# Moving the combinations of w_in to VectorE in the last row, with another order of steps in the first and the last pair of tiles

## The chip, the cores and the metric

The kernel runs on one core of a Trainium2 chip. Times are device microseconds of one execution; 0.2% of this kernel's time is 2.3 us. The engines are named as in the profile: PE is TensorE, PEld its weight loads, ACT ScalarE, DVE VectorE, POOL GpSimd, SP the engine that issues the transfers.

## The reference

Three stages follow one another. Attention between 8 batches of 512 tokens (8 heads of 64) and 32 state vectors per head, in both directions, gives 544 rows of 512 numbers per batch. A gated layer (512 to 1536 to 512) and then a second layer (512 to 1024 to 512, with a softmax-weighted activation and a normalisation) work on all rows:

```python
gate = 1.0 / (1.0 + np.exp(-(x @ w_gate)))
x = gate * (x @ w_val) @ w_out
h = x @ w_in
e = np.exp(h - np.max(h, axis=-1, keepdims=True))
solu = h * (e / (np.sum(e, axis=-1, keepdims=True) + 1e-09))
mu, var = mean and variance of solu over a row
out = ((solu - mu) / np.sqrt(var + 1e-06) * g_ln) @ w_out2
```

The weights and two of the outer inputs are 64-bit numbers, which the kernel converts on the chip (class Conv: three steps on VectorE and one integer add on GpSimd per block of 128x512).

## The kernel before

**Precision.** Each operand of a matmul is held as a high and a low half (tiles ...h and ...l, or xe and xo for w_in). A product takes three matmuls (mm3, lines 138 to 140): high by high and the two mixed ones. ScalarE makes the high half with a copy (hi_of, line 129), VectorE or GpSimd the low half with a subtraction (lo_of, line 135; GpSimd on lines 232, 618, 652 and 775).

**The rows.** The first two stages are worked through in nine rows (eight batches of 512 tokens, and one of the 256 state rows), the last of them for batch 7. A row is a loop over twelve chunks of 128 of the 1536 hidden columns (line 1037). In chunk c, TensorE makes the gate's product into the bank gps and the value's into vps (first_mm, 12 matmuls together), and then the output products of chunk c-1 into acc (out_acc, 12 matmuls). ScalarE takes the sigmoid of gps (sigma, L560), VectorE multiplies it with vps (gated, L564), ScalarE and VectorE split the result (gated_hi L129, gated_lo L570). A split of the precomputed state weights for later chunks runs in between (make, mh and ml, L129 and L135). In the last row a step of the conversion of w_out2 is added in chunks 2 to 10 (conv.step): rescaled halves of the block before (woh L234 on ScalarE, wol L235 on VectorE), the two ScalarE reads of the next (L195, L196), three VectorE steps (L203, L206, L213) and the integer add on GpSimd (L223). After the twelfth chunk come a dummy Exp that loads the table (line 1082), the output products of chunk 11, the splits of the four banks of the result (put, line 1085) and the first h products (h2_mm, 24 matmuls for tile 0).

**The steps on w_in.** h = x @ w_in is computed for pairs of 128-row tiles by seven products instead of eight (product, numbers 1 to 7, each of 6 matmuls). They need differences of blocks of w_in: T1 = B12 - B11, T3 = B22 - B12, T2 = B22 - T1 and T4 = B21 - T2, for two halves k of the contraction. w_pair_ops lists the 24 steps for this: 8 joins (high plus low half back to one number), 8 subs and 8 splits (a high half on ScalarE, a low half). The last row takes two of them off the list at the end of each chunk (lines 1079 to 1081), after everything else of that chunk in each engine's queue. Joins, subs and low halves are on GpSimd. The order of the list is written out by hand, and so is that of the row: the engines take their instructions in the order of the program.

**The second layer.** Four tiles of the last row (first) are taken singly, 24 matmuls each; then pairs (line 1128). For a pair, o, v and w are three PSUM banks (banks(i)), used in turn with three others: product 1 goes to o, which is copied to tmp; product 2 to v and v + tmp is tile i's first half of h; products 5 to w, which is copied to tmp (L1149), 6 onto o, copied to u2 (L1151), 3 onto w; w + u2 is tile i's second half. Product 7 goes onto o; o + tmp is the second half of tile i+1 (plus, L696, into v), and product 4 onto o gives its first half. h_max (L693) takes the maxima, chain(i) the exponentials (ScalarE, L716) and statistics (VectorE, L719 to L721), centre(i) subtracts the mean (ScalarE, L728 or L731), turn(i) transposes (VectorE and two transfers through DRAM, lines 762 to 768; on TensorE for the last two tiles, L756), halves(i, q) splits the transposed tile (ScalarE L129, GpSimd L775), row_scale(i) computes the factor of each row (VectorE, and two small instructions on GpSimd), out2(i) multiplies with w_out2 (24 matmuls, in two halves), and store(i) scales and writes. The work on the previous pair, i-2 and i-1, stands between the products of the current one:

```python
            halves(i - 2, 0)
            halves(i - 2, 1)
            row_scale(i - 2)
            product(i, 5, w, True, False)
            act(tmp, w, AF.Copy)
            product(i, 6, o, False, False)
            act(u2, o, AF.Copy)
            product(i, 3, w, False, True)
```

The first pair is i = 4, the last i = 32 (end); for the last, product 7 is issued ahead of chain(i), while the sum of its result stays behind chain(i) and half of the output products of tile i-2.

Of the kernel before, what the change touches and what calls it, by code (L numbers as in the profile page):

```python
# [14 lines left out]
ALU = mybir.AluOpType  # L15
# [11 lines left out]
def attn_moe_moe2_kernel(ctx: ExitStack, tc: tile.TileContext, x, state, w_gate, w_val, w_out, w_in2, w_out2, g_ln, out):  # L27
# [93 lines left out]
    vec = nc.vector  # L121
    pool = nc.gpsimd
    act = nc.scalar.activation

    def r(ap):
        return ap.bitcast(F32)
# [445 lines left out]
    def out_acc(c, n):  # L572
        h, l = woh[c], wol[c]
        i = c % 2
        for m in range(KC):
            sl = slice(m * P, (m + 1) * P)
            mm3(ps_acc(m, n), h[:, sl], l[:, sl], gh[i][:, 0:n], gl[i][:, 0:n], c == 0, c == NF1 - 1)
# [58 lines left out]
    def w_pair_ops(bf):  # L636

        join, sub, split = [{} for _ in range(3)]
        for k in range(2):
            b = dict(zip(("B11", "B12", "B21", "B22"), bf[4 * k:4 * k + 4]))  # L640

            def do_join(n, k=k, b=b):
                h, l = win(k + 2 * (n[1] == "2"), int(n[2]) - 1)
                pool.tensor_tensor(out=b[n], in0=r(h), in1=r(l), op=ALU.add)

            def do_sub(o, x, y, b=b):
                pool.tensor_tensor(out=b[o], in0=b[x], in1=b[y], op=ALU.subtract)

            def do_split(n, x, k=k, b=b):
                h, l = ts[n, k]  # L650
                hi_of(h, b[x])
                pool.tensor_tensor(out=l, in0=b[x], in1=r(h), op=ALU.subtract)

            for n in b:
                join[n, k] = partial(do_join, n)
            for n, x, y in (("T1", "B12", "B11"), ("T3", "B22", "B12"), ("T2", "B22", "B11"), ("T4", "B21", "B22")):
                o = {"T1": "B11", "T3": "B12", "T2": "B22", "T4": "B21"}[n]
                sub[n, k] = partial(do_sub, o, x, y)
                split[n, k] = partial(do_split, n, o)
        steps, late = [], []  # L660
        for k in range(2):
            steps += late[:1] + [join["B11", k], join["B12", k], sub["T1", k], join["B22", k], split["T1", k], sub["T3", k]]
            steps += [sub["T2", k], join["B21", k], split["T3", k], split["T2", k], sub["T4", k]]
            late = [split["T4", k]]
        steps += late
        return steps
# [9 lines left out]
    def h2_out(i, f):  # L676
        if tiles[i][0] == 0:
            return acc[2 * (i % 2) + f]
        a, b, c = banks(i)
        return ((b, c), (a, b))[i % 2][f]  # L680

    def product(i, n, o, start, stop):
        q, b, t = tiles[i]
# [11 lines left out]
    def plus(o, x, y):  # L695
        vec.tensor_tensor(out=o, in0=x, in1=y, op=ALU.add)  # L696
# [313 lines left out]
    with tc.manual_schedule():  # L1010
        for n_b, b in enumerate(blocks[1:], 1):
# [25 lines left out]
            for c in range(NF1):  # L1037
# [39 lines left out]
                elif (b == SREAD or last) and c > 1:  # L1077
                    conv.step(1)
                if last:
                    for _ in range(2):  # L1080
                        w_steps.pop(0)()
        act(stat[0][:, 0:1], half, AF.Exp)
        out_acc(NF1 - 1, S)
        for k in range(KC):
            ends = put(ps_acc(k, S), *yhl(0, k))
        for k in range(KC):
# [40 lines left out]
    with tc.manual_schedule():  # L1127
        for i in range(len(first), nt, 2):
# [13 lines left out]
                store(i - 3)  # L1142
            plus(v, v, tmp)
            h_max(i, 0)
            halves(i - 2, 0)
            halves(i - 2, 1)
            row_scale(i - 2)
            product(i, 5, w, True, False)
            act(tmp, w, AF.Copy)  # L1149
            product(i, 6, o, False, False)  # L1150
            act(u2, o, AF.Copy)  # L1151
            product(i, 3, w, False, True)
            next_ops(q, ops, step, n)
            plus(w, w, u2)
            h_max(i, 1)
            if end:
                product(i, 7, o, False, False)
            chain(i)
            halves(i - 1, 0)
            halves(i - 1, 1)  # L1160
            out2(i - 2, half1)
            if not end:
                product(i, 7, o, False, False)
            plus(v, o, tmp)
            h_max(i + 1, 1)
            centre(i)
            if end:
                product(i, 4, o, False, True)
# [55 lines left out]
```

## Time and profile before

| what | before |
|---|---|
| median of 3 runs | 1135.21 us (1133.67 to 1135.47) |
| profiled execution | 1134.19 us |
| its span, first to last instruction | 1132.4 us |
| mean granted TensorE clock | 0.994 |
| PE busy | 1084.0 us, 96% |
| DVE busy | 766.7 us, 68% |
| ACT busy | 601.8 us, 53% |
| POOL busy | 418.7 us, 37% |

The predictions are made against the profiled execution; its time has 1.8 us outside of the span, and the median of the runs is 1.0 us above it. A timeline row gives the start in us from the beginning of the span, the duration in us, engine, line, operation, written and read tiles, and in brackets the idle time of the engine before it and what ended that. "x2" says that two instructions of one kind in a row are shown as one. The records of neighbouring instructions on an engine overlap by some 0.07 us.

### The profile page before, as it was taken

The numbers are of one execution on the slowest core, as the hardware profiler recorded it, in microseconds if no ns is written. First come the engines' busy times: TensorE is split into PE (matmuls) and PEld (weight loads), VectorE is DVE, ScalarE is ACT, GpSimd is POOL, SyncE is SP. The second block draws the span as 40 slices with busy tenths as digits, with TensorE's granted clock in tenths as the row PEclk, the third lists the DMA queues.
The fourth block names the chain that finished last, engine by engine and source line by source line (L and its number), as shares of the span: only waits on it lengthen the run. The fifth ranks groups of instructions, "written<-read, shape, count | busy, mean of one in ns | idle before, by whom it ended". The sixth has DMA issues, their size and how long they took to land.

```text
span 1132.4 us, 15911 instructions
## 1 busy us (share of the span) xinstructions
PE 1084.0 (96%) x5501; PEld 861.5 (76%) x5501; DVE 766.7 (68%) x1324; ACT 601.8 (53%) x1169; POOL 418.7 (37%) x469
## 2 busy tenths in 40 slices
PE   7887899999999999999999999889999999999998
PEld 5555567778878778778778997667788888888877
DVE  6999865467465575564574466877578778777773
ACT  6766445545444455443555354555565565655552
POOL 2776733300000000000000054676566667667550
PEclk9999999999999999999999999999999999999999
DMA  8763040331440431532412434311453543553431
GB/s 230 258 204 102 20 95 1 80 84 38 116 124 20 115 66 38 164 77 58 96 38 67 142 99 149 106 39 56 134 174 121 174 155 131 164 170 119 158 122 38
DMA packets 139601, 122.89 MB, mean 109 GB/s; under 512 B 71040, under 2 KB 111232, under 8 KB 139520
## 3 DMA queue, kind: packets, MB, share of 16 engines
q1 hardware_dynamic: 139520, 121.87, 36.8%
q8 instruction: 43, 0.70, 0.3%
q14 instruction: 38, 0.31, 0.1%
HBM read 78.32 MB, written 43.52 MB: 108 GB/s over the span
## 4 chain that ended last, share of the span: by engine, by line
PE 73%; DVE 14%; issue 3%; DMA 3%; POOL 2%; ACT 2%; SPq 1%; DVEq 0%; POOLq 0%; ACTq 0%
PE acc L138 10%; PE acc L140 10%; PE acc L139 10%; PE att L138 5%; PE att L140 5%; PE att L139 5%; PE gps L138 4%; PE gps L139 4%; PE gps L140 4%; PE vps L138 4%; PE vps L140 4%; PE vps L139 4%; DVE wf L213 2%; DVE wf L203 1%; DVE wf L206 1%
## 5 line engine op out<-in xcount | busy, mean ns | idle before, releaser
L138 PE MATMUL acc<-gh,woh 128*128 128x512 f32 (+1 forms) x432 | 168.7, 390 | 0.6 <-ACT gh L129 0.6
L564 DVE TENSOR_TENSOR sg<-vps,sg 128x512 f32<-128x512 f32 (+1 forms) x108 | 71.1, 658 | 141.7 <-PE vps L140 123.0
L139 PE MATMUL acc<-gl,woh 128*128 128x512 f32 (+1 forms) x432 | 164.6, 381 | 2.2 <-POOL gl L570 1.3
L140 PE MATMUL acc<-gh,wol 128*128 128x512 f32 (+1 forms) x432 | 164.3, 380 | 0.0
L560 ACT ACTIVATE sg<-gps 128x512 f32<-128x512 f32 (+1 forms) x108 | 61.6, 570 | 154.5 <-PE gps L140 150.0
L138 PEld LDWEIGHTS acc<-gh,woh 128*128 128x128 f32 x432 | 81.8, 189 | 31.9 <-issue 15.5
L256 POOL MEMSET xtr<- 32x256 f32 x18 | 5.4, 302 | 262.1 <-PE att L324 261.5
L139 PEld LDWEIGHTS acc<-gl,woh 128*128 128x128 f32 x432 | 81.9, 190 | 18.5 <-POOL gl L570 2.2
L775 POOL TENSOR_TENSOR wol<-ut,woh 128x512 fp32r<-128x512 f32 x48 | 61.6, 1299 | 87.7 <-ACT woh L129 85.8
L140 PEld LDWEIGHTS acc<-gh,wol 128*128 128x128 f32 x432 | 81.6, 189 | 16.1
L223 POOL TENSOR_TENSOR tt<-tt,xn 128x512 int32<-128x512 int32 x16 | 20.9, 1304 | 194.8 <-DVE tt L213 171.2
L129 ACT ACTIVATE gh<-sg 128x512 fp32r<-128x512 f32 (+1 forms) x101 | 60.5, 599 | 53.6 <-DVE sg L564 53.6
L138 PE MATMUL gps<-ah,mh 128*128 128x512 f32 x192 | 75.9, 396 | 9.3 <-ACT sg L560 4.1
L570 DVE TENSOR_TENSOR gl<-sg,gh 128x512 fp32r<-128x512 f32 (+1 forms) x97 | 76.3, 786 | 10.2 <-ACT gh L129 6.9
L135 DVE TENSOR_TENSOR ml<-gps,mh 64x512 fp32r<-64x512 f32 (+2 forms) x57 | 38.6, 678 | 63.1 <-ACT stg L129 51.0
L138 PE MATMUL att<-woh,woh 128*128 128x512 f32 (+1 forms) x204 | 80.1, 392 | 0.0
L139 PE MATMUL att<-wol,woh 128*128 128x512 f32 (+1 forms) x204 | 79.5, 390 | 0.0
L140 PE MATMUL att<-woh,wol 128*128 128x512 f32 (+1 forms) x204 | 79.5, 390 | 0.0
L129 ACT ACTIVATE mh<-gps 64x512 fp32r<-64x512 f32 (+2 forms) x53 | 31.2, 589 | 90.7 <-PE gps L140 60.4
L139 PE MATMUL gps<-al,mh 128*128 128x512 f32 x192 | 75.4, 393 | 1.7 <-DVE al L135 1.7
L138 PE MATMUL vps<-ah,mh 128*128 128x512 f32 x192 | 75.7, 395 | 1.1 <-DVE ml L135 1.1
L140 PE MATMUL gps<-ah,ml 128*128 128x512 f32 x192 | 75.4, 393 | 1.0 <-DVE ml L135 0.9
(431 smaller groups left out, 2900.0 us busy)
## 6 DMA issues: line engine op xcount, KB each, us to landing
usp<-ub SPq DMA_DIRECT2D x32, 512.0 KB, 2.6
ut<-usp SPq DMA_DIRECT2D x128, 128.0 KB, 2.9
msp<-stg SPq DMA_DIRECT2D x72, 128.0 KB, 2.3
stg<-msp SPq DMA_DIRECT2D x36, 256.0 KB, 2.9
out_dram<-sg SPq DMA_DIRECT2D x32, 256.0 KB, 3.0
xn<-in_x_dram SPq DMA_DIRECT2D x15, 512.0 KB, 5.3
e2t<-in_x_dram SPq DMA_DIRECT2D x96, 64.0 KB, 2.6
stge<-in_moe_w_out_dram SPq DMA_DIRECT2D x10, 512.0 KB, 4.0
```

Of the source, the lines that this page charges most:

```text
L129: return act(dst, src, AF.Copy)
L135: return vec.tensor_tensor(out=dst, in0=src, in1=r(hi), op=ALU.subtract)
L138: mm(o, lh, rh, start=start, stop=False, **kw)
L139: mm(o, lh, rl, start=False, stop=False, **kw)
L140: return mm(o, ll, rh, start=False, stop=stop, **kw)
L203: vec.tensor_scalar(out=t, in0=t, scalar1=EXP_LO, scalar2=EXP_HI, op0=ALU.max, op1=ALU.min)
L213: vec.scalar_tensor_tensor(out=tu, in0=hi, scalar=0xC0000000, in1=tu, op0=ALU.bitwise_and, op1=ALU.bitwise_or)
L223: pool.tensor_tensor(out=ti, in0=ti, in1=lo, op=ALU.add)
L560: act(sg[c % 2][:, 0:n], gps[:, 0:n], AF.Sigmoid)
L564: vec.tensor_tensor(out=g, in0=vps[:, 0:n], in1=g, op=ALU.mult)
L570: eng.tensor_tensor(out=gl[c % 2][:, 0:n], in0=sg[c % 2][:, 0:n], in1=r(gh[c % 2][:, 0:n]), op=ALU.subtract)
L775: pool.tensor_tensor(out=lv, in0=wv[:, 4 * q:4 * q + 4], in1=r(hv), op=ALU.subtract)
```

## The change

1. In w_pair_ops the joins, subs and low halves go from GpSimd to VectorE; the high halves stay on ScalarE.
2. The list of the 24 steps is reordered: the sub of a difference and its split fall into different chunks, T3's sub comes before T1's split, T3's split before B21's join, and T4's split of the first half follows the next B11. In chunk 11 one step is taken instead of two; the last, T4's split, is issued behind the output products of chunk 11.
3. In the first pair (i = 4), halves of tile 2 and row_scale of tile 2 are issued behind the copies to tmp and u2 (between product 6 and product 3) instead of ahead of product 5. In the other pairs nothing moves.
4. In the last pair, the sum of product 7's result goes to the bank acc[3] instead of v, and it and its maximum are issued right behind product 7, ahead of chain(i). h2_out knows the bank.

```diff
--- before.py
+++ after.py
@@ -641,15 +641,15 @@
 
             def do_join(n, k=k, b=b):
                 h, l = win(k + 2 * (n[1] == "2"), int(n[2]) - 1)
-                pool.tensor_tensor(out=b[n], in0=r(h), in1=r(l), op=ALU.add)
+                vec.tensor_tensor(out=b[n], in0=r(h), in1=r(l), op=ALU.add)
 
             def do_sub(o, x, y, b=b):
-                pool.tensor_tensor(out=b[o], in0=b[x], in1=b[y], op=ALU.subtract)
+                vec.tensor_tensor(out=b[o], in0=b[x], in1=b[y], op=ALU.subtract)
 
             def do_split(n, x, k=k, b=b):
                 h, l = ts[n, k]
                 hi_of(h, b[x])
-                pool.tensor_tensor(out=l, in0=b[x], in1=r(h), op=ALU.subtract)
+                vec.tensor_tensor(out=l, in0=b[x], in1=r(h), op=ALU.subtract)
 
             for n in b:
                 join[n, k] = partial(do_join, n)
@@ -659,8 +659,8 @@
                 split[n, k] = partial(do_split, n, o)
         steps, late = [], []
         for k in range(2):
-            steps += late[:1] + [join["B11", k], join["B12", k], sub["T1", k], join["B22", k], split["T1", k], sub["T3", k]]
-            steps += [sub["T2", k], join["B21", k], split["T3", k], split["T2", k], sub["T4", k]]
+            steps += [join["B11", k], *late, join["B12", k], sub["T1", k], join["B22", k], sub["T3", k], split["T1", k]]
+            steps += [sub["T2", k], split["T3", k], join["B21", k], split["T2", k], sub["T4", k]]
             late = [split["T4", k]]
         steps += late
         return steps
@@ -677,7 +677,7 @@
         if tiles[i][0] == 0:
             return acc[2 * (i % 2) + f]
         a, b, c = banks(i)
-        return ((b, c), (a, b))[i % 2][f]
+        return ((b, c), (a, acc[3] if i + 1 == len(tiles) else b))[i % 2][f]
 
     def product(i, n, o, start, stop):
         q, b, t = tiles[i]
@@ -1077,10 +1077,11 @@
                 elif (b == SREAD or last) and c > 1:
                     conv.step(1)
                 if last:
-                    for _ in range(2):
+                    for _ in range(min(2, len(w_steps) - 1)):
                         w_steps.pop(0)()
         act(stat[0][:, 0:1], half, AF.Exp)
         out_acc(NF1 - 1, S)
+        w_steps.pop(0)()
         for k in range(KC):
             ends = put(ps_acc(k, S), *yhl(0, k))
         for k in range(KC):
@@ -1142,27 +1143,36 @@
                 store(i - 3)
             plus(v, v, tmp)
             h_max(i, 0)
-            halves(i - 2, 0)
-            halves(i - 2, 1)
-            row_scale(i - 2)
+            def operand():
+                halves(i - 2, 0)
+                halves(i - 2, 1)
+                row_scale(i - 2)
+
+            if i > len(first):
+                operand()
             product(i, 5, w, True, False)
             act(tmp, w, AF.Copy)
             product(i, 6, o, False, False)
             act(u2, o, AF.Copy)
+            if i == len(first):
+                operand()
             product(i, 3, w, False, True)
             next_ops(q, ops, step, n)
             plus(w, w, u2)
             h_max(i, 1)
             if end:
                 product(i, 7, o, False, False)
+                plus(acc[3], o, tmp)
+                h_max(i + 1, 1)
             chain(i)
             halves(i - 1, 0)
             halves(i - 1, 1)
             out2(i - 2, half1)
             if not end:
                 product(i, 7, o, False, False)
-            plus(v, o, tmp)
-            h_max(i + 1, 1)
+            if not end:
+                plus(v, o, tmp)
+                h_max(i + 1, 1)
             centre(i)
             if end:
                 product(i, 4, o, False, True)
```

## Rows read from the trace of the kernel before

**Rows 1.** The page, part 1: busy us, share of the span, instructions, by engine.
```profile
PE 1084.0 (96%) x5501; PEld 861.5 (76%) x5501; DVE 766.7 (68%) x1324; ACT 601.8 (53%) x1169; POOL 418.7 (37%) x469
```

**Rows 2.** TensorE's waits from 685 to 770 us: total us, times, longest us.
```profile
PE gps L138 <- ACT sg L560: 4.1, 1, 4.1
PE acc L138 <- DVE ml L135: 3.0, 1, 3.0
PE gps L139 <- DVE al L135: 1.1, 2, 0.7
```

**Rows 3.** Window: length, PE, PEld, DVE, ACT, POOL busy (count), PEclk, DMA, GB/s.
```profile
765.00:770.00 5.00, 4.96 (x15) 3.96 (x16) 1.77 (x3) 2.55 (x8) 3.90 (x6) 0.66 0.00 0
```

**Rows 4.** VectorE's timeline, last row: start, duration us, line, operands [idle before].
```profile
684.35 2.79 DVE L135 TENSOR_TENSOR al<-ee,ah 128x512 fp32r<-128x512 f32 x2
...
699.04 0.69 DVE L564 TENSOR_TENSOR sg<-vps,sg 128x512 f32<-128x512 f32 x1 [3.36 <-PE vps L140]
...
704.48 0.69 DVE L564 TENSOR_TENSOR sg<-vps,sg 128x512 f32<-128x512 f32 x1 [1.83 <-PE vps L140]
...
727.46 0.69 DVE L564 TENSOR_TENSOR sg<-vps,sg 128x512 f32<-128x512 f32 x1 [3.81 <-ACT sg L560]
...
728.85 0.69 DVE L570 TENSOR_TENSOR gl<-sg,gh 128x512 fp32r<-128x512 f32 x1
...
731.11 0.69 DVE L213 SCALAR_TENSOR_TENSOR tt<-xn,tt 128x512 uint32<-128x512 uint32 x1
...
740.65 1.79 DVE L570 TENSOR_TENSOR gl<-sg,gh 128x512 fp32r<-128x512 f32 x1
...
744.97 0.69 DVE L213 SCALAR_TENSOR_TENSOR tt<-xn,tt 128x512 uint32<-128x512 uint32 x1
745.58 0.69 DVE L564 TENSOR_TENSOR sg<-vps,sg 128x512 f32<-128x512 f32 x1
...
752.49 0.68 DVE L564 TENSOR_TENSOR sg<-vps,sg 128x512 f32<-128x512 f32 x1
```

**Rows 5.** GpSimd's timeline, last row.
```profile
684.86 3.43 POOL L644 TENSOR_TENSOR bf<-xe,xo 128x512 f32<-128x512 f32 x2
...
740.12 1.76 POOL L647 TENSOR_TENSOR bf<-bf,bf 128x512 f32<-128x512 f32 x1
...
745.80 1.30 POOL L223 TENSOR_TENSOR tt<-tt,xn 128x512 int32<-128x512 int32 x1 [2.21 <-issue]
```

**Rows 6.** ScalarE's timeline, last row.
```profile
726.31 0.63 ACT L129 ACTIVATE T4h<-bf 128x512 fp32r<-128x512 f32 x1 [6.26 <-POOL bf L647]
...
761.63 0.63 ACT L129 ACTIVATE T4h<-bf 128x512 fp32r<-128x512 f32 x1 [3.37 <-POOL bf L647]
```

**Rows 7.** TensorE's timeline, first pair.
```profile
806.87 0.50 PE L138 MATMUL acc<-xe,ys5h 128*128 128x512 f32 x1 [1.14 <-ACT stg L1149]
```

**Rows 8.** ScalarE's timeline, first pair.
```profile
805.19 1.15 ACT L129 ACTIVATE woh<-ut 128x512 fp32r<-128x512 f32 x2 [5.04 <-DMA ut<-usp]
```

**Rows 9.** TensorE's timeline, last pair.
```profile
1101.29 0.39 PE L140 MATMUL att<-woh,wol 128*128 128x512 f32 x1
1103.78 0.52 PE L138 MATMUL acc<-T4h,mh 128*128 128x512 f32 x1 [2.10 <-DVE acc L696]
...
1106.66 0.63 PE L139 MATMUL att<-wol,woh 128*128 128x512 f32 x1
1107.09 0.62 PE L140 MATMUL att<-woh,wol 128*128 128x512 f32 x1
...
1107.78 0.40 PE L139 MATMUL att<-wol,woh 128*128 128x512 f32 x1
...
1115.95 0.60 PE L756 MATMUL gps<-ident,ub 128*128 128x128 f32 x4
```

**Rows 10.** VectorE's timeline, last pair.
```profile
1103.06 0.67 DVE L696 TENSOR_TENSOR acc<-acc,stg 128x512 f32<-128x512 f32 x1
```

**Rows 11.** ScalarE's timeline, last pair.
```profile
1114.25 1.15 ACT L731 ACTIVATE ub<-xn,stat 128x1024 f32<-128x1024 f32 x1
```

## The prediction

> **What bounds the kernel now.** The page comes first: TensorE is busy for 1084.0 us, 96% of the span [rows 1]. Little is left to win, and only where TensorE stands idle or runs at its lower clock. So I read the list of TensorE's waits, limited to the last row (the last pass over the twelve chunks, some 685 to 765 us) [rows 2]: 4.1 us for a sigmoid on ScalarE, 3.0 us for the first split of the row's result, and 1.1 us at its head. These 8.2 us are what the first part of the change can reach, with what they cost behind them. A window shows that price: from 765 to 770 us, behind the 3.0 us, the granted clock is 0.66 [rows 3], that is, mostly the lower level, 1.2 instead of 2.4 GHz.
>
> The timelines of VectorE and GpSimd say why the row is late. At first VectorE waits for TensorE: the gated product of chunk 3 starts 5.44 us after that of chunk 2, TensorE's own pace of 24 matmuls at 0.227 us [rows 4]. From chunk 4 on VectorE sets the pace. The same split takes 0.69 us at 728.85 us and 1.79 us at 740.65 us, where it ends at 742.44 us, 0.56 us after GpSimd's subtraction of 740.12 us ended (741.88) [rows 4, 5]: it stood still until GpSimd was through. At the head of the row two VectorE splits take 2.79 us and two GpSimd sums 3.43 us, one in turn with the other [rows 4, 5]. The stall of 4.1 us comes in at ScalarE: its high half of T4 had waited 6.26 us for a subtraction on GpSimd, with the next sigmoid queued behind it [rows 6]. At the end of the row that happens again: 3.37 us of waiting for T4, then a table load, and only then the split that TensorE needs [rows 2, 6].
>
> The Trainium skill (SBUF — State Buffer, Who interferes with whom) calls this an exclusive lock between VectorE with two SBUF inputs and a GpSimd instruction that reads SBUF: who issues first has it for the whole instruction. The trace agrees, with the 0.56 us above.
>
> **The last row, step by step.** All 24 steps (8 sums, 8 differences, 8 splits' low halves) leave GpSimd for VectorE; GpSimd keeps one conversion add per chunk. The order changes so that each high half on ScalarE reads a difference of the chunk before, and the last T4 split moves behind the output products of the last chunk.
>
> Head: the two GpSimd sums that came between the two VectorE splits are gone; the GpSimd instruction ahead of the first split stays. Of the two waits, 1.1 us with a longest of 0.7, the longer goes [rows 2]: 0.8 us with the refill of TensorE's pipeline. Chunk 2's gated product then starts at 699.04 - 0.8 = 698.2 us [rows 4].
>
> Chunks 2 to 9: with GpSimd nearly silent, a chunk takes VectorE 731.11 + 0.61 - 727.46 = 4.26 us, where 0.61 us is the pitch from one instruction to the next (744.97 to 745.58) [rows 4]. Two steps add 1.22 us. VectorE on such sums is not in the trace; the nearest row, the split with both operands in SBUF, gives 0.69 us alone as the lower bound and 1.79 us against GpSimd as the upper [rows 4]. Against what do they run? The add is released 0.83 us after the conversion's last VectorE step starts (744.97 to 745.80); the first sum would start after 0.61 us [rows 4, 5]. So the sum goes first, the add next, and the second sum waits for it, as at the head: 1.79 - 0.69 = 1.10 us lost per chunk. Now the add hides beside the gated product, which has a PSUM operand; that cover is gone. A chunk is 4.26 + 1.22 + 1.10 = 6.58 us, still above TensorE's 5.44. Chunk 2 has no rescaled low half yet (0.67 us, taken like the split): 5.91 us. Chunk 10 starts at 698.2 + 5.91 + 7 x 6.58 = 750.2 us instead of 752.49 [rows 4]: **2.3 us** gained. That is little, because the work that VectorE takes on nearly replaces the waiting that it loses. TensorE's 4.1 us stall turns into several smaller waits, in chunks 7 to 11.
>
> From chunk 10 to the first product behind the row. Before: 12.5 us, from 752.49 us to the end of the 3.0 us wait, where the window of 765.0 us begins [rows 3]. After: chunk 10 holds VectorE for 1.39 us until its low half can start (as 727.46 to 728.85 [rows 4]), 0.61 for that, 0.67 for the rescaled half and 1.22 for two sums, 3.9 us; chunk 11 again 1.39 until its low half and 0.69 for it, 6.0 us; then 12 products at 0.227 us, 8.7 us. Meanwhile ScalarE loads its table and makes the T4 high half (0.63 us) and the first high half of the result, VectorE the low half (0.69), which is also there about 8.7 us after chunk 10's start. **3.8 us** gained. The T4 low half now stands on VectorE ahead of that low half; it hides, since that one waits for ScalarE anyway.
>
> The clock: with no idle stretch of 3 us at the end of the row, the 5 us at 0.66 run at full speed, worth 5 x 0.34 = 1.7 us. Engines behind it have little slack there, so I take **1.2 us**, bounds 0 and 1.7.
>
> The row: 2.3 + 3.8 + 1.2 = 7.3 us. Bounds: if every sum cost 1.79 us, a chunk would be 1.1 us longer still and chunk 10 would start 5 us later than now, not 2.3 earlier; if none lost anything, the row would be TensorE's: 698.2 + 8 x 5.44 + 48 x 0.227 = 752.6 us instead of 750.2 + 8.7 = 758.9, 6.3 us more gained.
>
> **The first pair.** TensorE waits 1.14 us for a copy on ScalarE [rows 7], and loses 0.3 us more, since idle time counts from the end of a matmul of 0.39 us whose successor could start after 0.227, and the first one then takes 0.50 [rows 7, 9]. That copy stood behind two high halves that had waited 5.04 us for a transfer [rows 8]. The change puts them behind both copies. They still start at 805.19 us with their transfer; the copies are done by then. What is late next is the low halves that GpSimd makes of them, which the products behind read; I leave 0.3 us for that. **1.1 us** gained, bounds 0 and 1.4. No DMA is moved; row_scale keeps its place among VectorE's and GpSimd's instructions.
>
> **The last pair.** TensorE waits 2.10 us for the last sum (VectorE, 1103.06 us), which stood behind the whole statistics chain of the other tile, since it overwrites that tile's bank [rows 9, 10]. With a bank of its own it runs as soon as product 7 ends, and is done before TensorE has finished the products it has in hand. From 1101.29 to 1107.78 us TensorE makes 11 steps of 0.227 us, 2.50 us of work, in 6.49 us, some of them 0.43 us apart [rows 9]: **4.0 us** gained, idle time and lower clock together. The price: sum and maximum (0.7 us each) now stand ahead of the chain, so the other tile is centred 1.4 us later; its transposes on TensorE come behind product 4 and 24 output products, 30 x 0.227 = 6.8 us, which cover it. What could be late next is the last tile's centring on ScalarE, from 1114.25 to 1115.40 us, 0.5 us ahead of TensorE's transposes at 1115.95 [rows 9, 11]; its own chain gets earlier with product 4, so the cover holds. Bounds 2.5 and 4.1.
>
> **The sum**: 7.3 + 1.1 + 4.0 = 12.4 us. The profiled execution took 1134.19 us, so 1121.8; the median of the runs, 1135.21, lies 1.0 above it: 1122.8 us.
>
> **Rivals.**
> (a) Both sums go ahead of the add, and the add falls beside the gated product as now. For it: the sums are queued back to back. Against it: at the head GpSimd got its turn between two VectorE splits [rows 4, 5]. A chunk is then 5.5 us, TensorE's pace, and up to 6.3 us more are gained: 1116.5 us. The page's rule (who issues first) leaves open which of two that wait is next.
> (b) VectorE's load eats the row: the add costs more than one turn, a chunk takes 6.9 us as now (gated products at 745.58 and 752.49 us [rows 4]), and chunk 10 starts no earlier. The end, the first and the last pair are left, 2.9 + 1.1 + 4.0 = 8.0 us: 1127.2 us. For it: VectorE has hardly any idle time in these chunks; against it: GpSimd is held to one instruction.
> (c) Slower: the clock. The smaller waits in chunks 7 to 11 may lie between 1.14 us, after which matmuls kept their pace, and 2.10 us, after which they came 0.43 us apart [rows 7, 9]. If the clock falls in chunk 8 and does not come back within the row, a chunk of 24 products takes 24 x 0.43 = 10.3 us instead of 6.58: four chunks lose 14.9 us and the last output products 2.4 us, so -12.4 + 17.3 = +4.9: 1140.1 us. It decides if a second idle stretch falls into the recovery. Against it: after the 2.10 us the matmuls were back at their pace within 4 us [rows 9], and VectorE's pace leaves room for that.
> (d) The change does not do what it says in the last pair: the later chain sets the end, and its 4.0 us stay. 1126.8 us. Against it: the 0.5 us of cover above.
>
> **How the numbers follow.** Forecast 0.64, (a) 0.14, (b) 0.10, (c) 0.05, (d) 0.07. The range goes from (a), 1116.5, to (b) and (d) with a little more loss, 1128.0; (c) and a corner where (b) and (d) meet stay out. A difference under 0.2% (2.3 us) can hardly be told from none here. Faster by more: 0.92; within, where (b) and (d) meet or the bounds do: 0.03; slower: 0.05, which is (c).
>
> **What would show it.** In the new profile: the wait for the sigmoid (4.1 us) and that for the first split (3.0 us) gone from TensorE's list; one step per chunk near 1.8 us and one near 0.7 us on VectorE; gated products about 6.6 us apart from chunk 3 on; the granted clock near 1.00 around the row's end and in the last pair; product 4 of the last pair without a wait. Wrong if both steps take the same time, if the pitch is 5.5 or 7 us, or if the last transposes of the kernel wait for centring.

## The result, and the profile after

The changed kernel takes 1122.78 us (median of 4 runs, 1122.63 to 1124.73) against 1134.44 us before (4 runs, 1132.5 to 1135.47): a ratio of 0.9903, with a 95% interval of 0.9885 to 0.9922, or 11.7 us less. Its profiled execution took 1122.80 us. The top of its page (columns as in [rows 1]):

```profile
span 1121.0 us, 15909 instructions
...
PE 1081.3 (96%) x5501; PEld 860.1 (77%) x5501; DVE 773.3 (69%) x1348; ACT 601.1 (54%) x1169; POOL 384.0 (34%) x445
```

GpSimd has lost 24 instructions and 34.7 us of busy time, VectorE has gained 24 instructions but only 6.6 us of busy time, and TensorE runs the same 5501 matmuls. The list of TensorE's waits from 680 to 770 us answers to [rows 2]:

```profile
PE gps L140 <- DVE ml L135: 3.2, 2, 1.6
PE gps L139 <- DVE al L135: 0.4, 1, 0.4
PE acc L139 <- DVE gl L570: 0.2, 1, 0.2
PE acc L138 <- ACT gh L129: 0.2, 1, 0.2
```

The waits for the sigmoid (4.1 us) and for the first split of the result (3.0 us) are gone, the head's 1.1 us is 0.4, and in their place stand two waits of 1.6 us for the split mh/ml. The granted clock behind the row, from the first h product on, answers to [rows 3]; in the last pair product 4 comes without a wait, against the 2.10 us of [rows 9]:

```profile
759.00:764.00 5.00, 5.00 (x23) 4.06 (x22) 1.79 (x3) 2.60 (x8) 3.77 (x6) 1.00 0.00 0
```

```profile
1093.73 0.40 PE L138 MATMUL acc<-T4h,mh 128*128 128x512 f32 x1
```

One chunk of the last row on VectorE, and GpSimd's add in it, answer to [rows 4, 5]:

```profile
737.41 0.68 DVE L564 TENSOR_TENSOR sg<-vps,sg 128x512 f32<-128x512 f32 x1
738.01 0.68 DVE L135 TENSOR_TENSOR ml<-stg,mh 128x512 fp32r<-128x512 f32 x1
738.78 0.69 DVE L570 TENSOR_TENSOR gl<-sg,gh 128x512 fp32r<-128x512 f32 x1
739.40 0.75 DVE L235 SCALAR_TENSOR_TENSOR wol<-tt,glnt,woh 128x512 fp32r<-128x512 f32 x1
740.07 0.42 DVE L203 TENSOR_SCALAR tt<-tt 128x512 f32<-128x512 f32 x1
740.52 0.43 DVE L206 TENSOR_SCALAR tt<-tt 128x512 uint32<-128x512 uint32 x1
740.98 0.69 DVE L213 SCALAR_TENSOR_TENSOR tt<-xn,tt 128x512 uint32<-128x512 uint32 x1
741.59 0.68 DVE L647 TENSOR_TENSOR bf<-bf,bf 128x512 f32<-128x512 f32 x1
742.20 1.79 DVE L652 TENSOR_TENSOR T1l<-bf,T1h 128x512 fp32r<-128x512 f32 x1
743.91 0.68 DVE L564 TENSOR_TENSOR sg<-vps,sg 128x512 f32<-128x512 f32 x1
```

```profile
741.81 1.63 POOL L223 TENSOR_TENSOR tt<-tt,xn 128x512 int32<-128x512 int32 x1 [4.88 <-DVE tt L213]
```

Every instruction takes 0.42 to 0.75 us, but for the chunk's second step: the low half of T1 takes 1.79 us. In each of the chunks 2 to 9, the ones with an add, the second step takes 1.79 to 1.81 us. The first step (L647, 741.59) starts ahead of the add (741.81), which stretches to 1.63 us (1.30 in [rows 5]); the second step stands until the add is through at 743.44 us and ends 0.55 us after it. The gated products are 6.50 us apart.

To see where the time went I set the stages of the traces side by side, each from the start of the last gated product ahead of the last row (683.83 us before, 684.84 us after; the 1.0 us between them comes about ahead of anything that the change touches and is left out in this way: TensorE's matmuls lie 1.7 us later from some 15 us on, and 0.7 us of that goes again between 640 and 668 us. Over all the executions of the table this start lies between 682.76 and 686.16 us). The table has the start times of six later events less that start, the last of them the instruction that scales the last result; the rows below the first two are the experiments.

| us from that start to | gated, chunk 10 | first h product | first T1 product | product 4, first pair | T1 product, last pair | last store |
|---|---|---|---|---|---|---|
| before | 68.66 | 81.20 | 113.48 | 131.41 | 409.49 | 444.41 |
| after | 65.58 | 74.21 | 106.29 | 123.07 | 400.68 | 431.69 |
| gpsimd_new_order | 67.39 | 78.42 | 110.45 | 127.30 | 404.92 | 435.92 |
| old_order | 65.66 | 75.65 | 107.69 | 124.25 | 403.70 | 434.71 |
| no_first | 65.61 | 74.24 | 106.41 | 124.89 | 404.19 | 435.20 |
| no_last | 65.62 | 74.25 | 106.38 | 123.15 | 401.79 | 435.16 |
| no_last_again | 65.58 | 74.22 | 106.34 | 122.99 | 400.90 | 435.87 |
| only_last | 68.66 | 81.21 | 113.55 | 131.94 | 409.55 | 440.56 |
| before_again | 68.89 | 81.44 | 113.52 | 131.47 | 409.63 | 444.60 |
| steps_first | 60.92 | 69.66 | 101.81 | 118.50 | 396.12 | 427.12 |
| spread | 61.00 | 70.19 | 102.07 | 118.71 | 396.33 | 427.33 |
| steps_first_spread | 59.14 | 68.48 | 100.40 | 116.98 | 395.82 | 426.83 |
| row_scale_scalar | 65.60 | 74.26 | 105.00 | 121.59 | 400.73 | 431.73 |
| best | 59.14 | 68.48 | 99.20 | 115.74 | 393.67 | 424.67 |

Stage by stage the change gains 3.08 us up to chunk 10, 3.91 from there to the first h product (12.54 against 8.63), 0.20 to the first T1 product, 1.15 in the first pair, 0.47 in the pairs between, and 3.91 in the last pair: 12.72 us. The pairs between run the same instructions in both; their length is between 277.6 and 279.5 us in the executions of the table, so that the 0.47 can't be told from their spread.

### The profile page after: what moved, and what is told of

It is laid out like the page before. It is cut to its first block, busy times and chain, and to the rows that moved or that the text cites. A ratio compares the mean times of both kernels' runs of the same rounds, so it can differ in the third digit from the quotient of the medians.

```text
span 1121.0 us, 15909 instructions
## 1 busy us (share of the span) xinstructions
PE 1081.3 (96%) x5501; PEld 860.1 (77%) x5501; DVE 773.3 (69%) x1348; ACT 601.1 (54%) x1169; POOL 384.0 (34%) x445
## 4 chain that ended last, share of the span: by engine, by line
PE 78%; DVE 13%; issue 3%; ACT 2%; DMA 1%; POOL 1%; SPq 0%; DVEq 0%; POOLq 0%; ACTq 0%
PE acc L138 11%; PE acc L140 10%; PE acc L139 10%; PE att L138 6%; PE att L140 6%; PE att L139 6%; PE gps L138 4%; PE gps L139 4%; PE gps L140 4%; PE vps L138 4%; PE vps L140 4%; PE vps L139 4%; DVE wf L213 2%; DVE wf L203 1%; DVE wf L206 1%
## 5 line engine op out<-in xcount | busy, mean ns | idle before, releaser
L223 POOL TENSOR_TENSOR tt<-tt,xn 128x512 int32<-128x512 int32 x16 | 23.5, 1466 | 215.5 <-PE vps L140 153.3
L570 DVE TENSOR_TENSOR gl<-sg,gh 128x512 fp32r<-128x512 f32 (+1 forms) x97 | 68.1, 702 | 10.9 <-ACT gh L129 6.9
```

Of the source, the lines that this page charges most:

```text
L223: pool.tensor_tensor(out=ti, in0=ti, in1=lo, op=ALU.add)
L570: eng.tensor_tensor(out=gl[c % 2][:, 0:n], in0=sg[c % 2][:, 0:n], in1=r(gh[c % 2][:, 0:n]), op=ALU.subtract)
```

## The experiments

The medians below are set beside the changed kernel's 1122.78 us, though they were taken at other times and on several chips. The 95% intervals of the ratios of the single undos (no_last 0.9900 to 0.9956, no_first 0.9881 to 0.9941, old_order 0.9882 to 0.9933) overlap with the changed kernel's (0.9885 to 0.9922), so what each is worth is read from its stage in the table.

**One part undone at a time.** The first two runs take back the last and the first pair.

```diff
-        return ((b, c), (a, acc[3] if i + 1 == len(tiles) else b))[i % 2][f]
+        return ((b, c), (a, b))[i % 2][f]
...
-                plus(acc[3], o, tmp)
-                h_max(i + 1, 1)
...
-            if not end:
-                plus(v, o, tmp)
-                h_max(i + 1, 1)
+            plus(v, o, tmp)
+            h_max(i + 1, 1)
```

> The changed kernel with the last pair as it was before (the sum of product 7 into v, behind the chain). Theory: the wait of 2.1 us and the half-rate matmuls behind it come back, everything else stays: 3.9 us slower than the changed kernel, about 1126.7 us, and product 4 again 6.5 us for 11 steps. Rival: the last pair was bounded by the later chain anyway and the 3.9 us at the end belong to work shifted from the row: less than 1 us slower, about 1123.5 us.

Measured: 1126.19 us (1123.33 to 1129.79, 5 runs), 3.4 us over the changed kernel. The wait is back, the half-rate stretch isn't. TensorE's timeline at product 4 and the window behind it (columns as in [rows 3]):

```profile
1093.28 0.39 PE L140 MATMUL att<-woh,wol 128*128 128x512 f32 x1
1095.77 0.50 PE L138 MATMUL acc<-T4h,mh 128*128 128x512 f32 x1 [2.10 <-DVE acc L696]
1096.11 0.40 PE L139 MATMUL acc<-T4l,mh 128*128 128x512 f32 x1
1096.34 0.39 PE L140 MATMUL acc<-T4h,ml 128*128 128x512 f32 x1
```

```profile
1096.00:1099.60 3.60, 3.60 (x17) 2.90 (x17) 1.95 (x8) 0.31 (x1) 0.40 (x1) 1.00 0.00 0
```

The matmuls are 0.23 us apart right behind the same 2.10 us of waiting, at a granted clock of 1.00, and the last pair takes 33.37 us (401.79 to 435.16), between the 31.01 of the changed kernel and the 34.92 of before. So the rival falls (2.4 us are lost in that very stage), and the theory is right on the wait and not on the clock; the section on the clock below comes back to it.

```diff
-            if i > len(first):
-                operand()
+            operand()
             product(i, 5, w, True, False)
...
-            if i == len(first):
-                operand()
```

> The changed kernel with the first pair as it was before (halves and row_scale ahead of product 5). Theory: product 3 waits again behind ScalarE's transfer-bound high halves: 1.0 to 1.4 us slower than the changed kernel, about 1124.0 us, with a TensorE wait of 1.0 to 1.2 us for the copy. Rival: the shift of 1.1 us at that place came from elsewhere (the transfer itself arriving earlier): no wait there, same time within 0.3 us.

Measured: 1125.17 us (1123.77 to 1125.37, 4 runs), 2.4 us over the changed kernel. The table has 1.70 us of it in the first pair (124.89 - 106.41 against 123.07 - 106.29); the pairs between took 1.7 us longer in this execution, too. The wait is back, a little longer than before the change, and ScalarE's row says why, its high halves having waited 5.30 us for the transfer ahead of the copy (TensorE, then ScalarE):

```profile
800.20 0.50 PE L138 MATMUL acc<-xe,ys5h 128*128 128x512 f32 x1 [1.48 <-ACT stg L1153]
```

```profile
798.52 1.15 ACT L129 ACTIVATE woh<-ut 128x512 fp32r<-128x512 f32 x2 [5.30 <-DMA ut<-usp]
799.57 0.58 ACT L1153 ACTIVATE stg<-acc 128x512 f32<-128x512 f32 x1
```

The theory holds; the wait and the stage's loss were each some 0.3 us above its upper bounds (1.2 and 1.4 us).

**Engine or order.** Two runs separate the two halves of the last row's change.

```diff
-            steps += [join["B11", k], *late, join["B12", k], sub["T1", k], join["B22", k], sub["T3", k], split["T1", k]]
-            steps += [sub["T2", k], split["T3", k], join["B21", k], split["T2", k], sub["T4", k]]
+            steps += late[:1] + [join["B11", k], join["B12", k], sub["T1", k], join["B22", k], split["T1", k], sub["T3", k]]
+            steps += [sub["T2", k], join["B21", k], split["T3", k], split["T2", k], sub["T4", k]]
...
-                    for _ in range(min(2, len(w_steps) - 1)):
+                    for _ in range(2):
...
         out_acc(NF1 - 1, S)
-        w_steps.pop(0)()
```

> The changed kernel with the steps in the old order and two per chunk to the end, still on VectorE. Theory: the engine was what mattered, not the order: VectorE's pitch stays 6.5 us per chunk, no 4 us stall in chunk 6, since VectorE ends a difference within 1 us; only the last T4 split, again ahead of the row's last splits, costs TensorE about 1.2 us at the end of the row: 1.2 us slower (0.5 to 2) than the changed kernel, 1124.0 us. Rival: the order (high halves a chunk apart) is what removed the stall: ScalarE waits again with the sigmoid behind it, TensorE waits 2 us or more in chunk 6 and 12: 4 us slower or more, 1127 us.

Measured: 1124.54 us (1123.48 to 1125.13, 4 runs), 1.8 us over the changed kernel. Up to chunk 10 the row is the same (65.66 against 65.58 us); 1.36 us are lost between there and the first h product (9.99 against 8.63 us), where ScalarE waits for the last T4 with the table load behind it:

```profile
756.39 0.63 ACT L129 ACTIVATE T4h<-bf 128x512 fp32r<-128x512 f32 x1 [1.36 <-DVE bf L647]
757.05 1.28 ACT L1082 ACT_TABLE_LOAD   x1
```

The theory holds: there is no 4 us stall in chunk 6, and TensorE's wait for the first split behind the row is 1.2 us. So with the steps on VectorE the order of the list does nothing that shows up to chunk 10; by these rows it is the place of the last split that costs behind it, though no run moved that alone.

```diff
-                vec.tensor_tensor(out=b[n], in0=r(h), in1=r(l), op=ALU.add)
+                pool.tensor_tensor(out=b[n], in0=r(h), in1=r(l), op=ALU.add)
...
-                vec.tensor_tensor(out=b[o], in0=b[x], in1=b[y], op=ALU.subtract)
+                pool.tensor_tensor(out=b[o], in0=b[x], in1=b[y], op=ALU.subtract)
...
-                vec.tensor_tensor(out=l, in0=b[x], in1=r(h), op=ALU.subtract)
+                pool.tensor_tensor(out=l, in0=b[x], in1=r(h), op=ALU.subtract)
```

> The changed kernel with its new order, all 24 steps back on GpSimd. Theory: the 4.1 us stall of ScalarE goes by the order alone, but VectorE and GpSimd block each other three times per chunk again: gated products 6.9 us apart, chunk 10 starts 2 us later than in the changed kernel, and the last T4 split is about 1.7 us late at the end of the row: 4 to 6 us slower than the changed kernel, about 1127.8 us. Rival: the order did it all, the engine is indifferent since VectorE loses as much to its own work as it did by waiting: within 1 us of the changed kernel.

Measured: 1126.57 us (1125.67 to 1127.21, 4 runs), 3.8 us over the changed kernel; by the table 1.8 us at chunk 10 and 4.21 at the first h product. TensorE's list from 683 to 775 us:

```profile
PE gps L140 <- DVE ml L135: 2.5, 2, 1.3
PE acc L139 <- DVE gl L570: 2.5, 3, 1.1
PE acc L138 <- DVE ml L135: 1.5, 1, 1.5
```

The theory holds, with gated products 6.9 us apart again and a loss near its lower bound of 4 us. The 4.1 us stall is gone by the order alone (and by the engine alone, as old_order showed), and 2.5, 2.5 and 1.5 us of smaller waits stand in its place, all for VectorE, whose splits take 1.48, 1.78 and 1.77 us in such a chunk, as before. The four combinations reach the first h product after 81.20 us (GpSimd, old order), 78.42 (GpSimd, new), 75.65 (VectorE, old) and 74.21 us (VectorE, new): the engine is worth 5.6 us in the old order and 4.2 in the new one, the order 2.8 us on GpSimd and 1.4 on VectorE.

**One turn of the lock.** If the second step only waits for the add, a place for the add beside the gated product should shorten the row.

```diff
+                if last:
+                    for _ in range(min(2, len(w_steps) - 1)):
+                        w_steps.pop(0)()
                 if b == SREAD and c == 0:
...
                 elif (b == SREAD or last) and c > 1:
                     conv.step(1)
-                if last:
-                    for _ in range(min(2, len(w_steps) - 1)):
-                        w_steps.pop(0)()
```

> The changed kernel with the two steps of a chunk ahead of the conversion's step instead of behind it, so that GpSimd's add runs beside the next gated product (PSUM operand) again. Theory (one turn of the lock): no step of a chunk takes 1.8 us any more, the split behind the gated product takes up to 1.5; VectorE's pitch falls from 6.5 to 5.4 to 6.2 us, TensorE's two waits of 1.6 us in chunks 8 and 10 shrink or go: 2 to 4.4 us faster than the changed kernel, 1119 to 1121 us. Rival (VectorE's own load is what bounds the row, the long step is only where its backlog shows): the pitch stays at 6.5 us and the time at 1122.8.

Measured: 1118.7 us (1116.64 to 1119.37, 4 runs), a ratio to before of 0.9864 (0.9842 to 0.9887) and 4.1 us under the changed kernel. VectorE and GpSimd in one chunk:

```profile
721.68 0.68 DVE L564 TENSOR_TENSOR sg<-vps,sg 128x512 f32<-128x512 f32 x1
722.28 1.48 DVE L135 TENSOR_TENSOR ml<-stg,mh 128x512 fp32r<-128x512 f32 x1
723.68 0.68 DVE L570 TENSOR_TENSOR gl<-sg,gh 128x512 fp32r<-128x512 f32 x1
724.28 0.68 DVE L652 TENSOR_TENSOR T4l<-bf,T4h 128x512 fp32r<-128x512 f32 x1
724.89 0.68 DVE L644 TENSOR_TENSOR bf<-xe,xo 128x512 f32<-128x512 f32 x1
...
727.67 0.68 DVE L564 TENSOR_TENSOR sg<-vps,sg 128x512 f32<-128x512 f32 x1
```

```profile
721.90 1.31 POOL L223 TENSOR_TENSOR tt<-tt,xn 128x512 int32<-128x512 int32 x1 [4.68 <-DVE tt L213]
```

Both steps (724.28, 724.89) take 0.68 us. The add runs at 1.31 us beside the gated product, which it doesn't slow (0.68), and then holds up the split behind it, 1.48 instead of 0.68 us: the turn is still there, but costs 0.80 us instead of 1.11, and some 0.2 us that VectorE lost ahead of the low half gl (738.01 to 738.78 above, against 0.60 from one instruction to the next) hide under it. Chunks are 5.99 us apart while the backlog lasts, and the first h product comes 4.55 us earlier. VectorE's work in the row was the same, so its load alone was not the bound, and the rival falls.

```diff
-                    for _ in range(min(2, len(w_steps) - 1)):
+                    for _ in range((2, 5, 1, 2, 1, 2, 1, 2, 1, 2, 2, 2)[c]):
```

(with the first half's T2 difference ahead of T1's split in the list.)

> The changed kernel with the 24 steps spread over the chunks as 2, 5, 1, 2, 1, 2, 1, 2, 1, 2, 2, 2 and one at the end, instead of two each: chunk 1 has VectorE idle for 2 us, and a chunk with one step has no second one to wait for the add. Theory (one turn of the lock): chunks with one step take VectorE about 4.9 us, those with two 6.5, so the row goes at TensorE's pace of 5.44 to 5.7 us: 3 to 4 us faster than the changed kernel, about 1119.3 us, and the one step of such a chunk takes 0.69 us. Rival (the add costs VectorE a turn wherever it is): the step or the instruction behind it takes 1.8 us in these chunks too, pitch about 5.9 on the mean: 1.5 us faster at most.

Measured: 1117.6 us (1117.53 to 1119.28, 4 runs), ratio 0.9860 (0.9843 to 0.9877). Chunks with one step and with two follow one another at 4.78 and 6.83 us (gated products at 721.80, 726.58 and 733.41 us), 5.8 on the mean. The single step takes 0.68 us, as the theory has it; the split behind the gated product then takes 1.20, which was the rival's point, and the mean pitch lies nearer to the rival's 5.9 than to the theory's 5.44 to 5.7. The medians differ by 5.2 us, more than either expected; by the table the gain is 4.2 us at the first T1 product (106.29 - 102.07) and 4.4 at the last store, and the rest is the spread of the medians.

The two edits together, the counts of spread in the place of steps_first:

> Both variants together: the steps ahead of the conversion's step, and 2, 5, 1, 2, 1, 2, 1, 2, 1, 2, 2, 2 and one of them per chunk. Theory: the row then goes at TensorE's own pace, 5.44 us per chunk (5.99 with two steps, less with one), no TensorE wait over 0.5 us between the head and the end of the row; since the row was within 1 us of that in either variant, 0 to 1 us faster than the better of the two: 1117.0 us. Rival: VectorE and the add still take turns and the gains do not add up, or the five steps of chunk 1 delay a split: 1118 us or more.

Measured: 1116.92 us (1116.39 to 1117.93, 4 runs), ratio 0.9837 (0.981 to 0.9864). TensorE's list from the head to 800 us has only two entries left, one of them behind the row:

```profile
PE acc L138 <- DVE xn L723: 1.0, 1, 1.0
PE gps L139 <- DVE al L135: 0.4, 1, 0.4
```

The median can't be told from spread's, but the trace shows the row: the first h product comes 1.18 us earlier than in steps_first (68.48 against 69.66), and from chunk 2's gated product to it TensorE makes 238 matmuls in 54.29 us, 0.228 us each. That is TensorE's own pace, the end that the prediction named for a row in which no sum loses anything (752.6 us, or 68.8 on the table's scale).

**The clock.** Two kernels were profiled again, and the last pair's change (the diff of no_last, reversed) was put alone into the kernel before.

> The kernel before, unchanged, for a second look at the clock behind its three long TensorE waits. Theory: the granted clock after a wait of 2.1 us is not fixed by the kernel: the stretch behind product 4 of the last pair can come out at 1.00 as well as at 0.53, while those behind 4.1 and 3.0 us of waiting are low again. Rival: a kernel's clock is the same in every execution: 0.53 there again, 34.9 us from the last T1 product to the last store.

> The kernel of the run without the last pair's part, unchanged, for a second look at the clock behind the 2.1 us wait. Theory: it can come out low here (35 us from the last T1 product to the last store) as well as high (33.4 us as in its first profile). Rival: high again, always 33.4 us, as the row ahead decides it.

Windows behind the three long waits of the kernel before in its second profile (4.0, 3.0 and 2.1 us); behind product 4 in its first profile; and there in the second profile of the run without the last pair's part:

```profile
727.80:731.20 3.40, 3.40 (x9) 2.64 (x8) 2.88 (x5) 2.84 (x5) 0.32 (x1) 0.50 0.09 34
763.90:768.90 5.00, 4.70 (x20) 3.87 (x21) 2.04 (x4) 2.82 (x9) 3.63 (x6) 1.00 0.00 0
1102.80:1106.40 3.60, 3.55 (x10) 2.82 (x11) 1.98 (x6) 0.59 (x1) 0.17 (x1) 0.66 0.00 0
```

```profile
1103.90:1107.50 3.60, 3.60 (x9) 2.83 (x10) 1.48 (x4) 0.42 (x1) 0.00 (x0) 0.53 0.00 0
```

```profile
1097.70:1101.30 3.60, 3.60 (x11) 2.86 (x12) 2.01 (x8) 0.37 (x1) 0.13 (x2) 0.65 0.00 0
```

Behind 4.0 us the clock is at half as in the first profile (0.51 there from 728.6 to 732.0 us), behind 3.0 us it stays full this time (0.66 in [rows 3]), behind 2.1 us it falls in three of four profiles (0.53, 0.66 and 0.65, but 1.00 in no_last above). The last pair took 34.92, 34.97, 33.37 and 34.97 us in these four. So a wait of 2 or 3 us may cost the clock or not, in executions of one kernel; what decides was not tried. no_last_again came out low, where its rival had it high. In before_again the last pair came out low again, as its rival had it, but behind 3.0 us the clock stayed full, where theory and rival both had it low; that the 2.1 us can go either way shows in no_last and no_last_again.

> The kernel before with the last pair's change alone (parts 1 to 3 left as they were). Theory: the wait of 2.1 us at product 4 goes whatever comes ahead of it, and with it the half-rate matmuls of the profiled execution of before: from the last T1 product to the last store's start 31.0 us instead of 34.9 in the profile, and a median 2.3 to 3.9 us under the kernel before. Rival: the gain there needs the earlier row (less backlog on VectorE): less than 1 us.

Measured: 1130.97 us (1129.88 to 1133.51, 10 runs), ratio 0.9970 (0.9956 to 0.9985): 3.8 us under the kernel before on the same chip. From the last T1 product to the last store it takes 31.01 us, as in the changed kernel. The part needs none of the others, and the rival falls.

**Where the clock's gain at the row's end went.** From the first h product to the first T1 product the changed kernel takes 32.08 us, before 32.28, though before ran the first 5 us at 0.66. Instead TensorE waits once more, for VectorE. TensorE's row, then VectorE's and GpSimd's just before it, in the changed kernel:

```profile
777.00 0.50 PE L138 MATMUL acc<-xe,mh 128*128 128x512 f32 x1 [1.16 <-DVE xn L719]
```

```profile
769.43 0.20 DVE L736 TENSOR_SCALAR stat<-stat 128x1 f32<-128x1 f32 x1
...
771.63 2.61 DVE L738 TENSOR_TENSOR stat<-stat 128x1 f32<-128x1 f32 x1
774.27 0.16 DVE L739 TENSOR_TENSOR stat<-stat 128x1 f32<-128x1 f32 x1
```

```profile
771.39 0.74 POOL L624 TENSOR_TENSOR e2t<-e2t,xtr 128x256 f32<-128x256 f32 x1
772.10 0.73 POOL L618 TENSOR_TENSOR ys3l<-xtr,ys3h 128x256 fp32r<-128x256 f32 x1
772.80 0.73 POOL L624 TENSOR_TENSOR e2t<-e2t,xtr 128x256 f32<-128x256 f32 x1
773.49 0.73 POOL L618 TENSOR_TENSOR ys3l<-xtr,ys3h 128x256 fp32r<-128x256 f32 x1
```

A product of two single numbers per partition (L738, both from SBUF) takes 2.61 us: it ends just after the fourth GpSimd instruction that ran meanwhile (773.49 + 0.73). In the first profile of the kernel before the same line takes 0.16 to 1.22 us. In its second profile, the one with the full clock behind the row, it takes 2.55 us in this place, and TensorE waits behind it:

```profile
776.77 2.55 DVE L738 TENSOR_TENSOR stat<-stat 128x1 f32<-128x1 f32 x1
```

```profile
782.09 0.50 PE L138 MATMUL acc<-xe,mh 128*128 128x512 f32 x1 [1.11 <-DVE xn L719]
```

So the stage takes 32.08 us in the unchanged kernel, too, when the clock doesn't fall: the half clock costs 0.2 us there (32.28), since the wait stands in for it. L736, whose second operand is a scalar, took 0.20 us at 769.43, in the middle of the same run of GpSimd work. So:

```diff
-        vec.tensor_tensor(out=s[:, 7:8], in0=s[:, 5:6], in1=s[:, 6:7], op=ALU.mult)
-        vec.tensor_tensor(out=s[:, 7:8], in0=s[:, 7:8], in1=s[:, 6:7], op=ALU.mult)
+        vec.tensor_scalar(out=s[:, 7:8], in0=s[:, 5:6], scalar1=s[:, 6:7], scalar2=s[:, 6:7], op0=ALU.mult, op1=ALU.mult)
```

> The changed kernel with the two one-element products of row_scale (two operands from SBUF) written as one instruction that takes the second factor as its scalar. In the changed kernel the first of these stood for 2.61 us at 771.6 us, until GpSimd ran out of work, while the one ahead of it, with a scalar operand, took 0.20 beside the same GpSimd work; TensorE then waited 1.16 us. Theory: that block is where the time gained at the row's end by the full clock was given back; it goes, TensorE's wait with it: from the row's end to the first T1 product 30.7 us instead of 32.1, and 1.0 to 2.0 us faster than the changed kernel, 1121.3 us. Rival: the stage is bound by the transfers of the first tiles, whatever VectorE does: 32.1 us again, same time within 0.4 us.

Measured: 1121.83 us (1120.37 to 1124.49, 4 runs). The new instruction takes 0.27 us:

```profile
770.43 0.27 DVE L738 TENSOR_SCALAR stat<-stat 128x1 f32<-128x1 f32 x1
```

TensorE has no wait left in that stage, which shrinks to 30.74 us (105.00 - 74.26): 1.34 us, where the theory had 1.4, and the rival falls. In the whole kernel 0.95 us show, less than the medians can tell apart, and in this execution the pairs between took 1.5 us longer than in the changed kernel's. The same edit on top of steps_first_spread:

> The row variants together (steps first, and spread) with the same edit of row_scale. Theory: the gains add up, since they lie in different stages: 1.0 to 2.0 us faster than that kernel's 1116.9, about 1115.5 us. Rival: no gain beyond it, 1116.9 us.

Measured: 1115.3 us (1114.23 to 1117.45, 4 runs), ratio 0.9838 (0.9817 to 0.9858), 7.5 us under the changed kernel and 1.6 under steps_first_spread. That last step lies within the noise of the two runs, but the stage shows it: 30.72 us (99.20 - 68.48) against 31.92.

## Why the prediction was right, and where not

**The whole**: 1122.8 us forecast, 1122.78 measured, and four of its five terms within 0.8 us. That the sum meets the median so closely is luck: two terms were off by 0.8 and 1.0 us in opposite directions, and the median of the kernel before, 1135.21 us when the forecast was made, came to 1134.44 with a fourth run, so that the medians differ by 11.7 us where the forecast took off 12.4.

- **The head and the chunks** (forecast 2.3 us, measured 3.08). The mechanism was as forecast: the first step goes ahead of the add, the second waits, 1.79 to 1.81 us, in chunks 2 to 9, and steps_first shows that this turn sets the pitch: 5.99 us with part of it under cover. The pitch was to be 6.58 us and is 6.50: VectorE's own instructions of a chunk, up to its first step, took 4.18 us (737.41 to 741.59) instead of 4.26. The head gave 1.03 us (15.21 to 14.18 us to chunk 2's gated product) instead of 0.8. Rivals (a) and (b) are out by the same rows: neither 5.5 nor 6.9 us. Two figures beside the sum don't come out of its rows: a loss of 1.1 us in each of eight chunks would start chunk 10 6.5 us later than before and not 5, and (b)'s 2.9 us for the row's end has no working, while its terms there are 3.8 and 1.2.
- **The 4.1 us stall** went, and TensorE's waits came back as two of 1.6 us, in chunks 8 and 10. The forecast had said so, but not which part does it; gpsimd_new_order and old_order show that the order and the engine each end the stall by themselves, and that the engine decides how much waiting comes in its place.
- **From chunk 10 to the first h product** (3.8, measured 3.91): the table shows both parts of it, 1.4 us for the order, by ScalarE's rows the last T4 split's place (9.99 us in old_order against 8.63), and 2.4 for the engine (11.03 in gpsimd_new_order).
- **The clock behind the row** (1.2, measured 0.2): the step that failed. The forecast took 1.2 of 5 x 0.34 us as gained and left 0.5 for "Engines behind it have little slack there". What followed at full clock was a single instruction of VectorE that GpSimd kept waiting for 2.61 us, and a TensorE wait of 1.16 us behind it; row_scale_scalar gives back 1.3 us. The kernel before does the same in its second profile, whose clock stayed at 1.00: 32.08 us against 32.28 with the drop. So the drop wasn't certain, and to be rid of it was worth 0.2 us in the unchanged kernel as well.
- **The first pair** (1.1, measured 1.15; 1.7 by undoing it): as forecast. The low halves, for which 0.3 us were left, show in no TensorE wait over 0.15 us.
- **The last pair** (4.0, measured 3.91): the wait of 2.1 us goes, and no centring takes its place; the transposes come 0.5 us behind it as before. But 1.6 of the 3.9 us hang on the clock, and in one of four profiles without the part the clock didn't fall. The part is then worth 2.36 us (33.37 - 31.01), just under the lower bound of 2.5.
- **Rival (c)**, the clock in the row: the two waits of 1.59 us were followed by matmuls at full pace in the changed kernel's profile. (d) is out by no_last and only_last.

The price of a chunk rests on VectorE and GpSimd taking turns. The Trainium skill (SBUF — State Buffer, Who interferes with whom) says that a VectorE instruction with two SBUF inputs contends with a GpSimd instruction that reads SBUF, and that one with at most one SBUF input, outside the two-port modes, doesn't. The trace of steps_first agrees: the add takes 1.31 us beside a gated product with a PSUM operand, which takes 0.68 us as without it. In one point the measurement goes beyond the page: it has the loser blocked for the whole of one instruction, and L738 above stood for four.

## What to carry to other kernels

Where VectorE and GpSimd share a stage, count who stands for whom, not how busy each is: moving 24 steps onto the busier engine paid here because it ended two of three turns per chunk, and starting the third beside an instruction with a PSUM operand paid 4 us more. An in-order engine that reads a late result just ahead of a step everyone needs (here ScalarE's high half ahead of the sigmoid) turns lateness into a stall; here a chunk of distance was enough. A gain at full clock behind one wait is worth counting only if the next stage isn't bound by something else.

## What had not been expected

- One-element VectorE instructions with two SBUF operands can be as dear as large ones beside GpSimd: 2.61 us for 128x1, through four GpSimd instructions of 0.73 to 0.74 us each, while splits of 128x512, and this line itself elsewhere (at most 1.22 us), got their turn after one. The same product with a scalar operand took 0.27 us. That is shown for one element only: a scalar form of 128x512 (L203) took 1.07 us at 669.27 us of the kernel before, beside a GpSimd split (668.76 to 670.06), and 0.41 us alone at 737.12. Why VectorE got no turn between those four was not tried.
- The granted clock behind an equal wait differs between executions of one kernel: 0.66 and 1.00 behind 3.0 us, 0.65 and 1.00 behind 2.1 us.
- The pairs between the first and the last took 277.6 to 279.5 us with the same instructions, and the work ahead of the last row ended over a range of 3.4 us: a spread that a single profile of this kernel can't see past.
